# Local attention and feed-forward on one core: first value tiles as 128-row products, wider first queries and keys, masks filled later, a new order

## The chip, the core and the metric

The kernel runs on one core of one Trainium2 chip. The metric is the device time of one execution in microseconds (us), as the median of the runs shown; smaller is better. The engines are TensorE (PE; PEld is its weight load), VectorE (DVE), ScalarE (ACT), GpSimd (POOL) and SyncE (SP, which only issues DMAs here). Each engine executes its own instructions in the order in which the program gives them, and waits for others on semaphores.

## The reference

Everything is bfloat16 with B, S, D = 1, 2048, 448, 16 heads of 28, and F = 1792. The result is x + s * g, where s is an attention over eight dilated positions and g a gated feed-forward, both of the normalised x.

```python
xn = _layernorm(x)                                   # no weights
qkv = (xn @ wqkv).reshape(B, S, 3, H, Dh)            # wqkv: 448 x 1344
idx = pos[:, None] - arange(8)[None, :] * 2          # positions p, p-2, ..., p-14
logits = einsum("bhsd,bhswd->bhsw", q, k[idx]) * Dh ** -0.5   # -1e9 where idx < 0
s = einsum("bhsw,bhswd->bhsd", softmax(logits), v[idx]).reshape(B, S, D) @ wo
h = gelu(xn @ w1 + b1)                               # 448 -> 1792
g = silu(h @ w2 + b2)                                # 1792 -> 448
return x + s * g
```

## The kernel before

**Tokens and tiles.** Tokens are reordered on loading, even positions first and odd ones after, so that the dilated window of a token is itself and the seven before it in its half. There are 16 tiles of 128 tokens; four tiles make a chunk of 512 (chunks 0 to 3). Of the 448 features, three blocks of 128 and one of 64 are contracted.

**Stages.** For each tile: statistics (L422, L426 on DVE), the reciprocal root (L434 on ACT and L437 on DVE for tiles 0 to 3; L443 and L444 on POOL for the others, several tiles together), the normalised `xn` (L456, DVE), and its transpose into `xnT`. For chunk 0 the transpose is done by PE against `ident` (L471) and copied out of the bank by DVE or ACT (L317, L315); later tiles are transposed by a DMA that SP issues (L380). Tile rows of `xn` are 512 wide: DVE copies the last 64 features a second time (L461). Per chunk, `project(c)` then makes values (`vproj`: 128 tokens by 448 columns) and, for four groups `g` of four heads, queries and keys (`qk_cols`: 120 columns by up to 512 tokens, L536). `values(b)` moves pieces of the value tiles into the layout that attention block b wants, by DMAs issued on POOL (L374). The feed-forward has `ff1` (14 products of 128 features by 512 tokens, with a Gelu on ACT, L609) and `ff2` (28 contraction steps, then bias, tanh and products on ACT and DVE). Attention works in nine blocks: scores (L747), exponentials on ACT (L757), a multiplication with a 0/1 mask (`m_gen`, `m_first`, `m_mid`; L764, on DVE or POOL), the product with the values (L780), and the division by the sum through two transposes on DVE (L791 to L805). `final` multiplies by wo (L490, L865), by the gate, adds x (L880) and stores (L884).

**Pairs.** Most products of PE run as 64x64 tiles: `pair(a, b)` works on two products at a time, with four matmuls side by side. In its first phase (16 matmuls) product a uses the upper 64 rows of the contraction and b the lower 64; in the second phase (12 matmuls) it is the other way round. Both write the same two banks, so the second phase waits until the first is done: a no-op on another engine's queue waits for the first phase's last matmul, and the second phase's first matmul waits for the no-op. The program calls it told, here it is the hop:

```python
        def f2(k):
            held["told"] = (nc.gpsimd if k.on == "POOL" else nc.sync).nop()
            behind(held["told"], held["last"][-1])
        told = plan.add(HOPS[0] if early else HOPS[1], 0.06, f2, [t], 300)
```

`HOPS` names POOL for both cases, so each hop stands in POOL's queue behind whatever the order puts ahead of it. In chunk 0 before, a value tile is one pair: its two halves of 224 columns. Queries and keys of groups 0 and 1 are made for 256 tokens at a time there, groups 2 and 3 for 512.

**The order.** `_Plan` is a list scheduler that runs when the program is built. Each step has engines it may run on, an assumed cost, dependences, a priority (`PRIO` by stage, `LATER` added for the steps behind a product) and the buffers it takes and gives (`p_b`: eight PSUM banks). It walks through time and picks, among the steps that could start first, the one of highest priority; steps allowed on two engines go where they would end first. The result is a fixed order on each engine. It also has an assumed delay for blocks of 128 weight-load and matmul pairs (`BLOCK`, `FETCH`). Warm-up matmuls (L330) fill PE until about 8 us in the plan.

**What POOL does at the start.** It fills `ident` (L337), loads b1, fills `own` (L343 to L347), `row0` and `wo` (L322), and then the three masks (L912 to L918), five instructions each; DVE widens the masks to eight copies (L923).

## Time and profile before

| | us |
|---|---|
| median of 3 runs | 161.62 (161.47 to 162.14) |
| profiled execution | 161.79 |
| its span | 160.1 |
| first real product (values of tile 0) on PE | 7.29 |
| first FF1 product on PE | 20.33 |
| first attention scores on PE | 55.00 |
| last matmul issued in the chain | 154.68 to 155.08 |

The profile is of one execution. The page's parts are the busy time of each engine, the span in 40 slices of 4 us (tenths of busy time), DMA queues, the chain of waits that ended last, and groups of instructions. In the chain, a line is start, duration and what was under way; "issue" is time in which the engine waited for nothing that the profile shows. In the list of busy time by stretches, each cell is the busy time of PE, PEld, DVE, ACT and POOL with the number of instructions, then the granted TensorE clock, the share of the DMA engines and GB/s. Names such as L490 are lines of the kernel before; numbers of the changed kernel lie up to 23 higher.

### The profile page before, as it was taken

The numbers are of one execution on the slowest core, as the hardware profiler recorded it, in microseconds if no ns is written. First come the engines' busy times: TensorE is split into PE (matmuls) and PEld (weight loads), VectorE is DVE, ScalarE is ACT, GpSimd is POOL, SyncE is SP. The second block draws the span as 40 slices with busy tenths as digits, with TensorE's granted clock in tenths as the row PEclk, the third lists the DMA queues.
The fourth block names the chain that finished last, engine by engine and source line by source line (L and its number), as shares of the span: only waits on it lengthen the run. The fifth ranks groups of instructions, "written<-read, shape, count | busy, mean of one in ns | idle before, by whom it ended". The sixth has DMA issues, their size and how long they took to land.

```text
span 160.1 us, 7978 instructions
## 1 busy us (share of the span) xinstructions
PE 149.5 (93%) x3535; PEld 100.7 (63%) x3535; DVE 117.8 (74%) x279; ACT 95.3 (60%) x173; POOL 58.8 (37%) x110
## 2 busy tenths in 40 slices
PE   6768699999999999999999999999999999999980
PEld 2456464555555667656987777666677766776570
DVE  6957572248951488988879999999459994597871
ACT  3337279755698773587837478657486598802020
POOL 6856274042382007520256663756003950000000
PEclk9999999999999999999999999999999999999997
DMA  4999469698028532010013230313110000002121
GB/s 144 283 289 316 101 101 121 106 377 277 19 60 128 105 66 80 26 53 4 17 45 95 79 86 14 92 61 104 58 61 4 6 4 4 4 0 61 57 86 33
DMA packets 18707, 14.52 MB, mean 91 GB/s; under 512 B 10037, under 2 KB 17891, under 8 KB 18672
## 3 DMA queue, kind: packets, MB, share of 16 engines
q1 hardware_dynamic: 13200, 7.20, 18.3%
q0 software_dynamic: 2368, 4.06, 11.0%
q10 hardware_dynamic: 3104, 2.75, 5.4%
q8 instruction: 27, 0.44, 1.2%
q14 instruction: 8, 0.07, 0.2%
HBM read 7.06 MB, written 1.84 MB: 56 GB/s over the span
## 4 chain that ended last, share of the span: by engine, by line
PE 81%; DVE 8%; POOL 5%; issue 3%; ACT 1%; POOLq 0%; ACTq 0%; DVEq 0%
PE bank L490 60%; PE bank L536 11%; PE bank L691 3%; PE bank L780 3%; PE bank L747 2%; DVE dt L800 1%; DVE xnT L805 1%; DVE dt L791 1%; DVE y L714 1%; POOL wo L322 1%; DVE g L724 1%; POOL m L916 1%; DVE qT L551 1%; POOL m L918 1%; PE bank L865 1%
## 5 line engine op out<-in xcount | busy, mean ns | idle before, releaser
L490 PE MATMUL bank<-xnT,w 64*64 64x512 bf16 x784 | 44.6, 376 | 0.0
L374 POOL DMA_DIRECT2D v<-v_tok x52 | 27.7, 537 | 44.2 <-PE bank L780 21.2
L490 PE MATMUL bank<-w,h 64*64 64x448 bf16 x784 | 40.4, 349 | 0.1
L609 ACT ACTIVATE h<-bank,b 128x512 bf16<-128x512 f32 x56 | 34.3, 688 | 8.3 <-PE bank L490 8.2
L490 PEld LDWEIGHTS <-w 64*64 64x64 bf16 x784 | 24.3, 107 | 16.5
L490 PEld LDWEIGHTS <-h 64*64 64x64 bf16 x784 | 25.2, 107 | 10.7 <-issue 0.2
L536 PE MATMUL bank<-xnT,w_in 64*64 64x512 bf16 (+1 forms) x504 | 28.2, 353 | 0.2
L549 ACT ACTIVATE qT<-bank,own 128x512 bf16<-128x512 f32 (+1 forms) x24 | 14.8, 651 | 11.4 <-PE bank L536 7.7
L536 PEld LDWEIGHTS <-w_in 64*64 64x64 bf16 x504 | 16.0, 107 | 7.9 <-issue 0.8
L720 ACT ACTIVATE t<-y 128x448 f32<-128x448 f32 x15 | 8.4, 578 | 19.4 <-DVE y L714 19.4
L757 ACT ACTIVATE E<-bank 128x456 bf16<-128x456 f32 (+1 forms) x36 | 17.0, 554 | 4.1 <-PE bank L747 4.1
L490 PEld LDWEIGHTS <-xnT 64*64 64x64 bf16 x408 | 13.3, 106 | 8.2 <-issue 2.5
L490 PE MATMUL bank<-w_in,xnT 64*64 64x448 bf16 (+1 forms) x280 | 14.4, 314 | 3.3 <-issue 1.8
L791 DVE STREAM_TRANSPOSE dt<-bank 128x480 f32<-128x480 f32 (+1 forms) x18 | 12.1, 670 | 4.5 <-PE bank L780 4.5
L764 POOL TENSOR_TENSOR E<-E,m_gen 128x456 bf16<-128x456 bf16 x10 | 10.3, 1054 | 12.0 <-ACT E L757 10.8
L800 DVE STREAM_TRANSPOSE dt<-rd 128x480 f32<-128x480 f32 (+1 forms) x18 | 12.1, 675 | 0.6
L456 DVE TENSOR_SCALAR xn<-x_sb,mv,rstd 128x448 bf16<-128x448 bf16 x16 | 6.6, 411 | 6.4 <-DMA xnT<-xn 4.0
L317 DVE CAST v_tok<-bank 128x448 bf16<-128x448 f32 (+1 forms) x8 | 4.3, 564 | 8.9 <-PE bank L490 8.9
L764 DVE TENSOR_TENSOR E<-E,m_gen 128x456 bf16<-128x456 bf16 (+1 forms) x22 | 9.1, 428 | 2.3 <-ACT E L757 2.0
L551 DVE TENSOR_SCALAR qT<-bank,own 128x512 bf16<-128x512 f32 (+1 forms) x12 | 7.6, 658 | 3.7 <-ACT qT L549 3.7
L714 DVE TENSOR_TENSOR y<-bank,b 128x448 f32<-128x448 f32 x15 | 8.7, 614 | 2.0 <-PE bank L490 1.4
L422 DVE BATCH_NORM_STATS2 st<-x_sb 128x6 f32<-128x448 bf16 x16 | 9.6, 605 | 0.8 <-DMA x_sb<-in_A_x_dram 0.8
(74 smaller groups left out, 165.1 us busy)
## 6 DMA issues: line engine op xcount, KB each, us to landing
v<-v_tok POOLq DMA_DIRECT2D x20, 96.0 KB, 3.1
out_dram<-o SPq DMA_DIRECT2D x15, 112.0 KB, 1.7
w<-in_B_w_dram ACTq DMA_DIRECT2D x2, 784.0 KB, 5.5
w<-in_B_w_dram SPq DMA_DIRECT2D x2, 672.0 KB, 9.2
x_sb<-in_A_x_dram ACTq DMA_DIRECT2D x2, 448.0 KB, 4.5
w_in<-in_A_wqkv_dram SPq DMA_DIRECT2D x4, 168.0 KB, 4.0
w<-in_B_w_dram SPq DMA_DIRECT2D x4, 112.0 KB, 8.5
x_sb<-in_A_x_dram SPq DMA_DIRECT2D x1, 448.0 KB, 7.0
```

What stands on the lines that cost most here:

```text
L374: nc.gpsimd.dma_start(dst(k), src())
L422: nc.vector.bn_stats(out=buf(p_st, k)[:], in_=x_sb[:, t, :])
L490: return [lambda c=c: nc.tensor.matmul(out[c:c + n], lhsT[:, c:c + n], rhs, start=start, stop=stop) for c in range(0, P, n)]
L536: return [lambda i=i: nc.tensor.matmul(ps[64 * i:64 * i + 64, :n], w[:, 2 * DH * i:2 * DH * i + 64], xnT[r, kt, cs], start=start, stop=sto ...
L549: nc.scalar.activation(qT[:, z, g, cs], buf(p_b, o, i)[:, :n], ACT.Copy, scale=own[:, z:z + 1])
L551: nc.vector.tensor_scalar(qT[:, z, g, cs], buf(p_b, o, i)[:, :n], own[:, z:z + 1], None, op0=ALU.mult)
L609: nc.scalar.activation(buf(p_h, own, i)[:], buf(p_b, own, i)[:], ACT.Gelu_apprx_tanh, bias=b1[:, mt:mt + 1])
L714: nc.vector.tensor_tensor(out=buf(p_y, k)[:, :n], in0=buf(p_b, own, i)[:, :n], in1=b2[:, cs], op=ALU.add)
L757: nc.scalar.activation(buf(p_E, k)[:, :n], buf(p_b, a, hl)[:, :n], ACT.Exp, scale=SCALE)
L764: (nc.gpsimd if k.on == "POOL" else nc.vector).tensor_tensor(out=E, in0=E, in1=m[:, :, :nq], op=ALU.mult)
L791: nc.vector.transpose(buf(p_dt, k)[:, :32 * m], buf(p_b, po, w)[:, :32 * m])
L800: nc.vector.transpose(buf(p_dt, d)[:, :32 * m].rearrange("p (b c) -> p b c", c=32), buf(p_rd, r)[:, :m].unsqueeze(2).to_broadcast((P, m, 32)))
```

## The change

Values of tiles 0 to 3 are made by the new `whole`: four matmuls of 128 rows (the last of 64) by 448 columns into one bank, one phase, no hop. The transposes of these tiles put the last 64 features twice into the bank themselves (five transposes instead of four), so DVE's second copy goes; tile 3 is normalised on ACT, with a small DVE product `nb` for its bias; the copies of `xnT` no longer wait for one another. In chunk 0 only group 0 of queries and keys is made in 256 tokens, group 1 now in 512. The loads of x tiles 2 and 3 both come before the query and key weights. The masks and the zero fill of `wo` wait for the fourth `xnT` tile in the plan, and come behind other steps on POOL. The warm-up plans 30 matmuls, the later ones of 256 columns instead of 128. `FETCH` and all numbers of `PRIO` and `LATER` are new, so the order changes everywhere. The tables are cut below.

```diff
--- before.py
+++ after.py
@@ -15,7 +15,7 @@
 SLACK = 0.12
 TABLE = 1.28
 SWITCH = 0.095
-BLOCK, FETCH = 128, ((0.0, 4.6), (40.0, 3.8))
+BLOCK, FETCH = 128, ((0.0, 5.4), (25.0, 4.0))
 SAME = 20
 HOPS = ("POOL", "POOL")
 MASK_ON = (("DVE", "POOL"), (0.4, 1.2))
@@ -253,6 +253,7 @@
     mv = sb("mv", [P, NT, 2], F32)
     sd = sb("sd", [P, NT], F32)
     rstd = sb("rstd", [P, NT], F32)
+    nb = sb("nb", [P, TPC], F32)
 
     def ring(name, n, shape, dt=BF16, fifo=False):
         return _Pool([sb(f"{name}{i}", shape, dt) for i in range(n)], fifo)
@@ -276,25 +277,26 @@
 
 
     PRIO = {
-        "qk": (39.5, 4, 213, 51, 92.5, 143, 200.5, 98, 50.5, 202, 197, 18, 151, 102.5, 140, 200.5,),
-        "values": (173, 201, 102, 152,),
...
+        "qk": (55.5, 79.5, 32, 67, 121.5, 80, 198.5, 81, 54.5, 156, 58, 3, 55.5, 172.5, 116.5,
+            115,),
+        "values": (126.5, 59, 64.5, 123,),
...
-    LATER = {"swap": 99.5, "qk": 74.5, "v": 42.5, "gelu": 77.5, "exp": -10.5, "mask": -47, "pv": 67.5, "recip": 33.5, "os": 175, "y": 205.5, "tanh": 154, "g": 68.5, "sg": 70.5, "o": 26.5}
+    LATER = {"swap": 125.5, "qk": 45, "v": 77, "gelu": 172, "exp": 192.5, "mask": -41.5, "pv": 83.5, "recip": 148.5, "os": 161.5, "y": 154, "tanh": 103, "g": 19.5, "sg": 58.5, "o": 206}
     plan = _Plan()
 
@@ -325,10 +327,10 @@
     warm = p_h.bufs[-1]
     t_on = plan.add("DMA", 0.8, lambda _: None, (), 100)
     t_warm = plan.add("DVE", 0.3, memset("vector", warm[:], 0.0), [t_on], prio=100)
-    for i in range(48):
-        def fn(k, n=512 if i < 9 else P):
+    for i in range(30):
+        def fn(k, n=512 if i < 9 else 256):
             nc.tensor.matmul(buf(p_b, k)[:, :n], warm[:, :P], warm[:, :n], start=True, stop=True)
-        t_warm = plan.add("PE", 0.43 if i < 9 else 0.107, fn, [t_warm], -1, take=(p_b,), limit=8.0)
+        t_warm = plan.add("PE", 0.43 if i < 9 else 0.215, fn, [t_warm], -1, take=(p_b,), limit=8.0)
         t_warm.give = ((p_b, t_warm, 0),)
     t_eps = plan.add("DVE", 0.07, memset("vector", eps_t[:], EPS), [t_on], prio=99)
     t_eps = plan.add("DVE", 0.07, memset("vector", half_t[:], -0.5), [t_eps], prio=99)
@@ -345,7 +347,6 @@
             nc.gpsimd.affine_select(out=own4[:], in_=own4[:], compare_op=ALU.is_ge, fill=0.0, base=op_base,
                                     pattern=[[-sign * DH, 2], [-sign * 64, 2]], channel_multiplier=sign)
         nc.gpsimd.tensor_tensor(out=own[:], in0=own4[:, :, 0], in1=own4[:, :, 1], op=ALU.add)
-    t_own = plan.add("POOL", 0.5, mk_own, [t_on], prio=94)
 
     def heads(v):
         return v.rearrange("p a (b c) -> p a b c", c=32)[:, :, 0:3:2, :]
@@ -358,7 +359,7 @@
 
     t_row0 = plan.add("POOL", 0.1, memset("gpsimd", row0[:], 0.0), [t_on], prio=93)
     t_row0 = plan.add("POOL", 0.1, memset("gpsimd", row0[:1, :], 1.0), [t_row0], prio=93)
-    t_wo = [plan.add("POOL", 1.0, memset("gpsimd", wo[:], 0.0), [t_on], prio=93)]
+    t_own = plan.add("POOL", 0.9, mk_own, [t_row0], prio=94)
 
     def dma(eng, dst, src, kb, prio, deps=(), issue=0.5, rate=350.0, tail=1.7, pieces=1):
         def fn(_):
@@ -405,7 +406,8 @@
             dma("ACT", w_in3[64:], tails[:, 1:3, :], 112, 298, rate=290.0, tail=1.45)]
     t_wqk = []
     for i in range(2):
-        load_x(2 + i, 1, 297 - 2 * i, "SP")
+        load_x(2 + i, 1, 297, "SP")
+    for i in range(2):
         t_wqk.append([load_w(w_in[:, :, c0:c0 + D // 2], A_wqkv[:KF, c0:c0 + D // 2], 296 - 2 * i) for c0 in (i * D // 2, D + i * D // 2)])
 
     t_b1z = plan.add("POOL", 0.1, memset("gpsimd", b1r[:], 0.0), [t_on], prio=99)
@@ -449,38 +451,46 @@
     def half_bank(ap):
         return ap[:].bitcast(BF16)[:, :512].rearrange("p (a b) -> p a b", a=4)
 
-    t_xT, t_xT01 = {}, {}
+    t_xT = {}
 
     def norm(t, prio):
         def f1(k):
             nc.vector.tensor_scalar(buf(p_xn, k)[:, :D], x_sb[:, t, :], mv[:, t, 0:1], rstd[:, t:t + 1],
                                     op0=ALU.subtract, op1=ALU.mult)
-        a = plan.add("DVE", 0.40, f1, [t_rs[t]], prio, take=(p_xn,))
+
+        def f0(_):
+            nc.vector.scalar_tensor_tensor(out=nb[:, t:t + 1], in0=mv[:, t, 0:1], scalar=-1.0, in1=rstd[:, t:t + 1], op0=ALU.mult, op1=ALU.mult)
+
+        def f1a(k):
+            nc.scalar.activation(buf(p_xn, k)[:, :D], x_sb[:, t, :], ACT.Identity, bias=nb[:, t:t + 1], scale=rstd[:, t:t + 1])
+        if t == 3:
+            a = plan.add("ACT", act(D), f1a, [plan.add("DVE", 0.12, f0, [t_rs[t]], 280)], prio, take=(p_xn,))
+        else:
+            a = plan.add("DVE", 0.40, f1, [t_rs[t]], prio, take=(p_xn,))
 
         def f2(_):
             nc.vector.tensor_copy(buf(p_xn, a)[:, D:], buf(p_xn, a)[:, KF:D])
-        twice = plan.add("DVE", 0.15, f2, [a], prio)
         if t >= TPC:
+            twice = plan.add("DVE", 0.15, f2, [a], prio)
             t_xT[t] = dma_T(xnT[:, :, t * P:(t + 1) * P], lambda: buf(p_xn, a)[:], [twice], PRIO["turn_x"][t], (p_xn, a, 0))
             return
         halves = []
         for i in range(2):
             def f3(k, i=i):
                 xn, tp = buf(p_xn, a), half_bank(buf(p_b, (halves or [k])[0]))
-                for kt in (2 * i, 2 * i + 1):
-                    nc.tensor.transpose(tp[:, kt, :], xn[:, kt * P:(kt + 1) * P], ident[:])
-            halves.append(plan.add("PE", 0.13 if t else 0.22, f3, [twice if i else a, t_ident] + halves, prio, take=() if i else (p_b,),
+                for kt, c0, n in ((0, 0, P), (1, 0, P)) if not i else ((2, 0, P), (3, 0, 64), (3, 64, 64)):
+                    nc.tensor.transpose(tp[c0:c0 + n, kt, :], xn[:, kt * P:kt * P + n], ident[:])
+            halves.append(plan.add("PE", (0.13 if t else 0.22) + 0.06 * i, f3, [a, t_ident] + halves, prio, take=() if i else (p_b,),
                                    give=((p_xn, a, 0),) if i else (), tail=0.15, pairs=2))
         b = halves[0]
 
         n = 2 if t < 2 else 4
+        done = []
         for k0 in range(0, KT, n):
             def f4(k, k0=k0):
                 copy(k.on, xnT[:, k0:k0 + n, t * P:(t + 1) * P], half_bank(buf(p_b, b))[:, k0:k0 + n, :])
-            t_xT[t] = plan.add(("DVE", "ACT"), (dve(n * P, 2), act(n * P)), f4, [halves[(k0 + n - 1) // 2]] + ([t_xT01[t]] if k0 else []), prio,
-                               give=((p_b, b, 0),) if k0 + n == KT else ())
-            t_xT01.setdefault(t, t_xT[t])
-
+            done.append(plan.add(("DVE", "ACT"), (dve(n * P, 2), act(n * P)), f4, [halves[(k0 + n - 1) // 2]], prio))
+        t_xT[t] = plan.add("SEM", 0.0, None, done, give=((p_b, b, 0),), tail=-HOP)
 
     def half_rows(half):
         return slice(64 * half, 64 * half + 64) if half < 2 else slice(0, P)
@@ -523,6 +533,13 @@
         a.evac(u, t, 0)
         b.evac(u, t, 1)
         return u
+
+    def whole(j, prio):
+        def f(k):
+            for kt in range(KT):
+                j.part(buf(p_b, k), kt, 2 if kt < 3 else 0, kt == 0, kt == 3)[0]()
+        a = plan.add("PE", pe(j.n, KT), f, j.deps + j.late, prio, take=(p_b,), tail=0.15, pairs=KT)
+        j.evac(a, a, 0)
 
     t_qk = [[] for _ in range(NT)]
 
@@ -566,6 +583,8 @@
         def part(ps, kt, half, start, stop):
             r = half_rows(half)
             w = w_in[r, kt, 2 * D + c0:2 * D + c0 + n] if kt < 3 else w_in3[r, 1, c0:c0 + n]
+            if t < TPC:
+                return [lambda: nc.tensor.matmul(ps[:, :n], xnT[r, kt, k0:k0 + P], w, start=start, stop=stop)]
             return strips(ps[:, :n], xnT[r, kt, k0:k0 + P], w, half, start, stop)
 
         def evac(a, own, i):
@@ -906,6 +925,32 @@
     rstds(4, 2)
     rstds(6, 2)
 
+    blocks_of = [[b for b, (q, n, _) in enumerate(VIS) if (q + 4 * n - 1) // CH == c] for c in range(NCH)]
+
+    def project(c):
+        pv = PRIO["values"][c]
+        for t in range(c * TPC, (c + 1) * TPC):
+            norm(t, PRIO["norm"][t])
+        for t in range(c * TPC, (c + 1) * TPC, 1 if not c else 2):
+            if c:
+                pair(vproj(t, pv), vproj(t + 1, pv), pv - 0.1 * (t % TPC), c < 2)
+            else:
+                whole(vproj(t, pv), pv - 0.1 * t)
+        for g in range(G):
+            q = PRIO["qk"][G * c + g]
+            for t in (range(0, TPC, 2) if not c and g < 1 else (c * TPC,)):
+                pair(*[qk_cols(w, g, t, CH // 2 if not c and g < 1 else CH, q) for w in range(2)], q - 0.1 * (t > 0), c < 2)
...
+    project(0)
+
+    t_wo = [plan.add("POOL", 1.6, memset("gpsimd", wo[:], 0.0), [t_xT[3]], prio=70)]
     t_mask = []
     for m, w1_, n, first in ((m_gen, m1[0], NW, None), (m_first, m1[1], NW, 0), (m_mid, m1[2], NW - 1, 1)):
         def fn(_, s=w1_, n=n, first=first):
@@ -917,34 +962,12 @@
                                         pattern=[[-1, n]], channel_multiplier=1)
                 nc.gpsimd.affine_select(out=a, in_=a, compare_op=ALU.is_ge, fill=0.0, base=BACK - back,
                                         pattern=[[1, n]], channel_multiplier=-1)
-        t_m = plan.add("POOL", 0.9, fn, [t_ident], prio=75)
+        t_m = plan.add("POOL", 1.45, fn, [t_xT[3]], prio=75)
 
         def fn(_, m=m, s=w1_, n=n):
             nc.vector.tensor_copy(m[:, :, :n], s[:, :n].unsqueeze(1).to_broadcast((P, 8, n)))
         t_mask.append(plan.add("DVE", 0.3, fn, [t_m, t_st[3]], prio=60))
 
...
-        for t in range(c * TPC, (c + 1) * TPC, 1 if not c else 2):
-            a = ((t, pv, 0, D // 2), (t, pv, D // 2, D // 2)) if not c else ((t, pv), (t + 1, pv))
-            pair(*[vproj(*j) for j in a], pv - 0.1 * (t % TPC), c < 2)
-        for g in range(G):
-            q = PRIO["qk"][G * c + g]
-            for t in (range(0, TPC, 2) if not c and g < 2 else (c * TPC,)):
-                pair(*[qk_cols(w, g, t, CH // 2 if not c and g < 2 else CH, q) for w in range(2)], q - 0.1 * (t > 0), c < 2)
...
-    project(0)
```

## The prediction

> **What bounds the kernel now.** I read the page first: its table of busy time, then the 40 slices.
>
> ```profile
> PE 149.5 (93%) x3535; PEld 100.7 (63%) x3535; DVE 117.8 (74%) x279; ACT 95.3 (60%) x173; POOL 58.8 (37%) x110
> ...
> PE   6768699999999999999999999999999999999980
> ...
> POOL 6856274042382007520256663756003950000000
> PEclk9999999999999999999999999999999999999997
> ```
>
> TensorE (PE) bounds the kernel: from slice six to the last two it never shows less than 9 tenths, at full granted clock. Time can come from two places: idle PE in the first five slices, or less PE work. So I next took the busy time by stretches (span's start to PE's first wait, and so on; each cell is busy us and count).
>
> ```profile
> 0.00:9.55 9.55, 5.86 (x47) 2.83 (x47) 6.99 (x37) 3.29 (x8) 7.41 (x30) 1.00 0.81 217
> 9.55:15.56 6.01, 6.01 (x177) 4.75 (x178) 4.50 (x15) 3.67 (x12) 3.39 (x7) 1.00 1.07 325
> 15.56:17.35 1.79, 0.00 (x1) 0.00 (x1) 0.99 (x2) 1.13 (x2) 0.52 (x1) 1.00 0.97 184
> 17.35:22.02 4.67, 4.67 (x116) 3.41 (x119) 2.95 (x9) 1.89 (x4) 2.20 (x5) 1.00 0.17 46
> 22.02:150.00 127.98, 127.56 (x3154) 85.31 (x3147) 97.06 (x205) 84.03 (x146) 45.24 (x69) 1.00 0.30 72
> ```
>
> In the body, 22.02 to 150, PE is idle for 0.42 us of 128; in the head one stretch of 1.79 us has no PE work at all, and before 9.55 only 47 matmuls ran, most of them warm-up. The chain of waits says why.
>
> ```profile
> 8.12 0.25 POOL m L918
> ...
> 9.21 0.23 POOL m L916
> 9.44 0.04 issue
> 9.48 0.03 POOLq L515
> 9.50 0.04 issue
> 9.55 0.86 PE bank L490 x28
> ...
> 15.47 0.09 PE bank L490
> 15.56 1.79 issue
> 17.35 0.48 PE bank L490 x11
> ```
>
> The first value pair ran its first phase at 7.29 to 7.8; its second waits for a no-op on POOL (the hop, L515), which stands in POOL's queue behind the fills of three masks (5.34 to 9.44). At 15.56 PE waits for nothing the profile shows. The page's list of DMA queues has a hint.
>
> ```profile
> q8 instruction: 27, 0.44, 1.2%
> q14 instruction: 8, 0.07, 0.2%
> ```
>
> These 0.51 MB over the span's 7978 instructions are 64 bytes each, and a packet of q8 (0.44 MB / 27 = 16 KB) is 256 instructions, 128 pairs of weight load and matmul. The stall falls at PE's pair 224, in the stretch where data DMA is fullest (share 1.07 just before). I read it as a late block of instructions; blocks then change at pairs 95, 223, 351.
>
> **What goes.** Values of tiles 0 to 3 were 4 x 28 matmuls 64x224 and become 4 x 4 of 128x448. Old price by the chain: 0.86 to 0.67 us for 28. New price: the nearest row is L691, 128x448, 14 in 2.75 us, 0.196 each, 0.79 a tile. So this edit saves no PE work (-0.1 to +0.1 a tile, nought taken); it removes four hops and 96 pairs. Group 1 of queries and keys at 512 columns removes 28 pairs and no streaming time (16 of 256 columns take 0.44, 16 of 512 take 0.86). Altogether 120 fewer pairs stand in the head, so the block boundary of pair 224 falls in FF1, whose 512-column matmuls last twice as long per pair.
>
> **The head, step by step** (order of each engine's instructions in the changed kernel, durations from rows before). x0's statistics, root and reciprocal are as now, to 4.76. Two rows of the timeline, of POOL and of DVE:
>
> ```profile
> 3.80 1.58 POOL L322 MEMSET wo<- 128x1792 bf16 x1
> ```
>
> ```profile
> 4.80 0.72 DVE L456 TENSOR_SCALAR xn<-x_sb,mv,rstd 128x448 bf16<-128x448 bf16 x1
> ```
>
> The other three normalisations of chunk 0 took 0.39 to 0.40; this one lay under the memset, which now comes later, so 0.40 is taken. In front of it DVE does an aggregate and two memsets (0.35): xn0 at 5.5, as now. Tile 1 follows at 6.1 (6.86 now, its 0.18 copy gone). ACT turns both into xnT by 7.3 (four copies, 0.33). Values 0 and 1 run from 6.5 to 8.1, behind 16 warm-up matmuls instead of 22 (PE kept clock 1.00 through gaps of 1.47 and 1.79 us; the longest below is 0.65). Their weights were used at 7.29 before, and by 4.0 us from issue at 1.25 to 1.85 land by 6.
>
> Tile 3 is now loaded ahead of the query/key weights, which are issued 0.54 later (its issue row) and land about 8.6 (issue 4.1 to 4.6 plus 4.0); phase one of group 0 takes 0.44, to 9.05. Its hop stands behind POOL's first value move, which waits for ACT's copy of value 0 (8.95: after the roots of tiles 2 and 3 at 8.35) and takes 0.55. So PE waits to 9.6 behind the transposes of tile 2 (9.05 to 9.4), runs phase two to 9.95, and the fifth transpose a tile costs 0.07 (8 took 0.55). Tile 3 is normalised on ACT (0.55 by a copy of 448 columns), behind two value copies: 10.1; transposes to 10.5, values 2 to 11.3. xnT3 stands on DVE behind a query copy that waits for ACT: 11.45; values 3 to 12.25; transposed b1 0.16. Group 1's weights are issued as now (5.2 at the latest, landing by 9.7), so they are there. Then 16+16+12 of 512 (2.37), 16 of 256 (0.44), 12 of 512 (0.65): FF1 starts at 15.9, instead of 20.33. Behind it are left 12 of 256 and one group of 28 (1.85 us); before, 24 of 256 (0.65). Gain: 20.33 + 0.65 - 15.9 - 1.85 = **3.2 us**.
>
> **What is given back.** (1) FF1's third pair needs bank 171, whose key copy DVE now does behind statistics of tiles 4, 5 and 7 (landed 14.45), two mask copies and a query copy: 14.45 + 2.2 + 0.3 + 0.7 + 0.3 + 0.65 = 18.6. PE is there at 17.96: **0.65** lost. (2) PE changes between 64x64 and 128-row products 12 times after its first values instead of 5 after 9.55 (the last six tiles' FF2 parts are interleaved with pairs). Eight transposes between pairs took 0.55 where 8 x 0.053 is 0.43, the one of b1 0.16: 0.05 to 0.06 a switch; the head's are in the rows used, six more in the tail make **0.3**. The Trainium skill, "TensorEngine Tiling (Array Packing)", Key Properties, says that changing the tiling mode drains TensorE: it speaks against this change, gives no figure, and free switches would leave 0.3 more.
>
> (3) Masks moved: 15 POOL instructions (5.34 to 9.74, 1.4 to 1.6 a mask) and wo's memset now follow five value moves, at 11.7 to 17.6. Behind them in that queue stand the hops of groups 1 and 2 and of the second 256 pair, one after each mask, at 13.2, 14.65 and 16.05; PE wants them at 14.1, 15.2 and 16.8. Then rstd of tiles 4 and 5 at 18.7. The cover is 0.6 us at least, so nothing is charged; each us by which POOL is later than that is a us of PE. Masks are first used after attention starts (55 now). The Trainium skill, "SBUF — State Buffer", Who interferes with whom, lets a POOL instruction shut out a VectorE one that uses both ports; the 0.72 row agrees, with 0.32 of it. By that rule the moved fills would cost at most the like once, since DVE has only short mask copies (0.27 to 0.34) of that kind under them.
>
> (4) Tiles 4 to 7 are still turned by SP (1.3 each, landing 3.7 from issue). xn4 comes at 20.2 as now, but xn7 by 22.5 instead of 25.8, so they land at 24.6 to 28.5; PE wants tiles 4 and 5 at 26.1, tiles 6 and 7 at 29.6. The margin is 0.2 and 1.1, no more.
>
> (5) ACT must have FF1's table (1.28) before its Gelus: 17.95 + 1.28 = 19.25, then 0.69 each, two in 1.38 against 1.5 of PE for a pair. It keeps up.
>
> (6) The body's order is new throughout. Its PE work is the same, and only 0.4 us idle and a slow place at 69.2 (16 matmuls in 1.53 instead of 0.86, 1.0 in all with what follows, behind DVE's outputs) could be better; eight mask products go from DVE to POOL (8 x 1.05 more there, 8 x 0.41 less on DVE), four final additions come back, and with the copies that change engine DVE has about 2 us less in all. Bounds: -1.0 (that place goes) to +8.4 (each mask holds a hop). I take 0, because ten such masks and 52 moves now share POOL's queue with the hops and the waits of PE name one hop, the first.
>
> Sum: 3.2 - 0.65 - 0.3 = **2.3 us**. The profiled execution took 161.79 us (span 160.1), 0.17 over the median of 161.62; its span would be 157.8 and its time 159.5, the median **159.3 us**. The tail after the last FF2 part (activation, two multiplications, addition, output) has the same links.
>
> **Rivals.** *Better by the body* (0.15): DVE's 2 us of relief removes the place at 69.2 and bank 171 comes in time: 1.6 more, 157.7. For it: attention starts after FF2 of fewer tiles, so more filler is left. Against: POOL's masks are slower (1.05 for 0.43).
> *The block is still late* (0.13): the block behind pair 95 took from 10.9 to 17.35, 6.45 us. Now pair 95 is reached at 13.1 and pair 223 at about 19.9, 6.8 later, so no stall; a block that comes a full 1.3 us later, say, gives 160.6.
> *PE waits for what feeds it* (0.10): if tiles 4 to 7 or the Gelus come no earlier than now, PE catches up with them at 26 to 30 and the whole gain is a wait: 161.6. Against: (4) and (5).
> *POOL's queue becomes the bound* (0.12), slower than before: hops of the pairs stand behind 18 masks of 1.05 instead of 10. It decides from 3.1 us of the 8.4 exposed (2.3 + 0.8); half exposed gives 159.3 + 4.2 = 163.5. Against: the single hop wait in 52 moves.
>
> **Numbers.** Forecast 0.50; with the first two rivals faster has 0.78, same 0.10, slower 0.12. About 0.8 us (0.5%) is what can be told from no change. The range, 157.5 to 161.8, holds all but the POOL case and the farther ends.
>
> **What would show it.** Right: no PE wait on a POOL hop before 9; no issue wait of over 0.5 us; first FF1 product at 15.5 to 16.5; a PE wait of about 0.6 on DVE's key copy at 18; PE's last matmul near 152.8 instead of 155.1. Wrong: FF1 after 18, or a body (FF1's start to the last matmul) with over 2 us of PE idle, above all behind POOL.

## The result: slower by 1.1%

The changed kernel takes **163.67 us** (median of 4 runs, 162.97 to 163.96) against 161.70 (161.47 to 162.14) for the kernel before beside it: a ratio of **1.0112** (95% interval 1.0073 to 1.0151). The forecast was 159.3, range 157.5 to 161.8. The profiled execution took 163.78, its span is 161.7. Some executions run a few us longer than the others of the same kernel; the ratios leave these out, the medians do not.

Page of the changed kernel, busy time and slices:

```profile
PE 153.1 (95%) x3409; PEld 103.1 (64%) x3409; DVE 121.3 (75%) x270; ACT 93.0 (57%) x168; POOL 63.6 (39%) x114
...
PE   6999889999999989999999999999999899999990
...
POOL 6047669262452880760589427532003550000000
```

PE has fewer instructions (3409 for 3535) and more busy time. The head is fuller, as forecast; but PE shows 8 tenths at slices 5 and 6 (16 to 24 us), 15 and 32, where the kernel before had 9 in every slice behind the fifth up to the last two. By stretches (cells as before):

```profile
0.00:7.56 7.56, 6.31 (x27) 3.00 (x28) 5.86 (x33) 2.90 (x7) 2.57 (x14) 1.00 0.76 204
7.56:9.47 1.91, 1.91 (x10) 0.59 (x7) 0.80 (x5) 1.32 (x5) 0.02 (x1) 1.00 1.01 283
9.47:17.11 7.64, 7.57 (x121) 3.98 (x124) 3.25 (x10) 3.85 (x8) 5.53 (x19) 1.00 1.01 296
17.11:22.02 4.91, 3.71 (x73) 2.11 (x69) 4.84 (x10) 3.43 (x6) 3.02 (x5) 1.00 0.08 21
22.02:150.00 127.98, 126.16 (x3085) 88.08 (x3081) 98.97 (x199) 79.64 (x140) 52.42 (x77) 1.00 0.32 75
```

FF1 starts at 17.11 (20.33 before), with no wait for a hop and no issue wait ahead of it. But PE is idle for 1.20 us from there to 22, and for 1.82 us of the 128 behind, where it was 0.42. The chain of waits at the first place:

```profile
17.72 1.65 DVE m_first L968
19.37 0.54 DVE st L424
19.91 0.02 issue
19.93 0.18 DVE mv L428
20.11 0.58 DVE kT L319
20.70 0.04 issue
20.74 7.53 PE bank L500 x135
```

PE's third FF1 pair waits for DVE's key copy (L319), and that stands behind a copy of a mask of which 1.65 us lie in this chain. (L968 is L923 of the kernel before: the lines of the mask fills and copies lie 45 higher, not up to 23.)

Busy time hides small waits, so for the rest I use one more measure: the time from each matmul's start to the next one's, less its streaming time at full clock (columns / 2400 us, a quarter of it for a 64x64 tile; the prediction's 0.86 for sixteen of 64x512 is this to within 0.01). I call the sum **excess**. It also holds the 2.5 to 2.6 us that the attention's short products (64x57) take beyond their columns, before and after alike, so what counts are differences between kernels.

| kernel | 0 to 20 us | 20 to 145 | after 145 | sum | last matmul starts |
|---|---|---|---|---|---|
| before | 7.59 | 5.69 | 0.31 | 13.59 | 155.19 |
| changed | 6.48 | 7.58 | 0.89 | 14.95 | 157.20 |

The last matmul starts 2.01 later: 0.64 of more streaming (values of four tiles 0.37, transposes 0.21, warm-up 0.05), 1.10 less excess in the head, 1.89 more in the body, 0.58 more in the tail. All later ratios are to the kernel before, run beside the same kernels.

### The profile page after: what moved, and what is told of

It is laid out like the page before. It is cut to its first block, busy times and chain, and to the rows that moved or that the text cites. A ratio compares the mean times of both kernels' runs of the same rounds, so it can differ in the third digit from the quotient of the medians.

```text
span 161.7 us, 7710 instructions
## 1 busy us (share of the span) xinstructions
PE 153.1 (95%) x3409; PEld 103.1 (64%) x3409; DVE 121.3 (75%) x270; ACT 93.0 (57%) x168; POOL 63.6 (39%) x114
## 4 chain that ended last, share of the span: by engine, by line
PE 73%; DVE 19%; ACT 3%; issue 2%; DVEq 0%; ACTq 0%
PE bank L500 48%; PE bank L553 11%; PE bank L710 3%; PE bank L332 3%; DVE dt L819 3%; PE bank L799 2%; DVE dt L810 2%; PE bank L587 2%; DVE y L733 2%; DVE w_in L743 2%; DVE E L783 1%; DVE sg L893 1%; DVE qT L568 1%; DVE xnT L824 1%; ACT E L776 1%
## 5 line engine op out<-in xcount | busy, mean ns | idle before, releaser
L500 PE MATMUL bank<-xnT,w 64*64 64x512 bf16 x784 | 46.4, 376 | 1.5 <-DVE kT L319 1.2
L500 PE MATMUL bank<-w,h 64*64 64x448 bf16 x784 | 41.1, 349 | 0.0
L500 PEld LDWEIGHTS <-w 64*64 64x64 bf16 x784 | 27.5, 107 | 16.4 <-issue 3.2
L553 PE MATMUL bank<-xnT,w_in 64*64 64x512 bf16 (+1 forms) x476 | 30.2, 364 | 0.5 <-DVE xnT L824 0.5
L783 POOL TENSOR_TENSOR E<-E,m_gen 128x456 bf16<-128x456 bf16 x17 | 18.6, 1120 | 23.1 <-ACT E L776 20.0
L568 DVE TENSOR_SCALAR qT<-bank,own 128x512 bf16<-128x512 f32 (+1 forms) x18 | 12.5, 714 | 14.1 <-PE bank L553 8.2
L566 ACT ACTIVATE qT<-bank,own 128x512 bf16<-128x512 f32 (+1 forms) x16 | 10.1, 659 | 11.5 <-PE bank L553 8.6
L500 PEld LDWEIGHTS <-xnT 64*64 64x64 bf16 x296 | 10.9, 107 | 4.9 <-issue 1.2
L500 PE MATMUL bank<-w_in,xnT 64*64 64x448 bf16 x168 | 10.8, 350 | 0.6 <-DVE xnT L824 0.6
L317 ACT CAST kT<-bank 128x512 bf16<-128x512 f32 (+1 forms) x15 | 8.3, 553 | 2.9 <-PE bank L500 2.3
L317 ACT CAST v_tok<-bank 128x448 bf16<-128x448 f32 x12 | 6.0, 541 | 4.9 <-issue 2.3
```

Of the source, the lines that this page charges most:

```text
L317: nc.scalar.copy(o, i)
L500: return [lambda c=c: nc.tensor.matmul(out[c:c + n], lhsT[:, c:c + n], rhs, start=start, stop=stop) for c in range(0, P, n)]
L553: return [lambda i=i: nc.tensor.matmul(ps[64 * i:64 * i + 64, :n], w[:, 2 * DH * i:2 * DH * i + 64], xnT[r, kt, cs], start=start, stop=sto ...
L566: nc.scalar.activation(qT[:, z, g, cs], buf(p_b, o, i)[:, :n], ACT.Copy, scale=own[:, z:z + 1])
L568: nc.vector.tensor_scalar(qT[:, z, g, cs], buf(p_b, o, i)[:, :n], own[:, z:z + 1], None, op0=ALU.mult)
L783: (nc.gpsimd if k.on == "POOL" else nc.vector).tensor_tensor(out=E, in0=E, in1=m[:, :, :nq], op=ALU.mult)
```

## The experiments

Two theories stood first. *Blocking*: POOL's moved memset and its eight additional mask products shut DVE out, and DVE's late copies hold PE's banks. *Order*: the new order's queue on DVE holds PE, whatever POOL does. Apart from experiments 10 and 11, every kernel keeps the finished order and moves, adds or leaves out only the named steps in it.

**1. The memset of wo in front again.**

```diff
     plan.run()
+    t_wo[0].deps = []
+    t_wo[0].start = t_own.start + 0.01
+    plan.order.sort(key=lambda t: (t.start, t.seq))
```

> One move in the changed kernel: the memset of wo goes back to the front of POOL's queue (right behind own), everything else in the same order. If POOL's memset is what held VectorE's copy of m_first (1.74 us where the other copies took 0.27) and through it the key copy that frees bank 171: m_first's copy takes 0.27 to 0.34, PE's wait of 1.21 in FF1 at 19.2 is gone or below 0.2, PE's last matmul comes 1.2 to 1.5 us earlier (157.2 to 155.8) and the time is 162.2 to 162.5. If VectorE's new order alone makes the key copy late: the wait stays at 0.7 or more and the time at 163.0 to 163.7. If the wait goes but a later one (tiles 4 and 5 at 26 to 31) takes it over: no wait at 19, a new one of about 1 us before 32, time 163.5.

162.72 us, ratio 1.0074 (1.0045 to 1.0102): 0.4% better than the changed kernel, less than the first expectation. DVE's timeline of the changed kernel, POOL's, and DVE's of this one:

```profile
17.63 1.74 DVE L968 COPY m_first<-m 128x456 bf16<-128x456 bf16 x1
```

```profile
17.65 1.59 POOL L324 MEMSET wo<- 128x1792 bf16 x1
```

```profile
17.30 0.27 DVE L968 COPY m_first<-m 128x456 bf16<-128x456 bf16 x1
17.49 0.62 DVE L424 BATCH_NORM_STATS2 st<-x_sb 128x6 f32<-128x448 bf16 x1
18.14 0.18 DVE L428 BATCH_NORM_AGGREGATE mv<-st 128x2 f32<-128x6 f32 x1
18.25 0.66 DVE L319 CAST kT<-bank 128x512 bf16<-128x512 f32 x1
```

The copy that ran beside the memset ended 0.13 after the memset's end; without it the copy takes 0.27, and the wait at 19 (excess 1.53) is gone. The third expectation came true in part: PE now waits at 29.8 (excess 0.84) for a DMA transpose of tiles 4 to 7.

**2. Besides, value tiles in one mode.**

```diff
-                j.part(buf(p_b, k), kt, 2 if kt < 3 else 0, kt == 0, kt == 3)[0]()
+                j.part(buf(p_b, k), kt, 2, kt == 0, kt == 3)[0]()
...
+                w = w if kt < 3 else w_v3[:]
...
```

> The kernel of the run before (memset of wo in front), and the last of the four products of each value tile 0 to 3 also takes 128 rows: its weights lie in a tile of their own whose lower 64 rows are zero (one more DMA on ACT's queue and one memset at the start), so TensorE keeps one mode through a value tile. If changing from 128 to 64 rows and back costs a drain: the fourth product takes 0.19 to 0.20 instead of 0.285 and the first of the next tile 0.19 instead of 0.29, 0.2 a tile; FF1 starts 0.4 to 0.8 us earlier than in the run before (tile 3's normalisation may eat half) and the time falls by 0.4 to 0.8, to about 161.8. If the two long products are long for another reason (clock, weights landing): they stay at 0.28 and the time is that of the run before within 0.2.

162.74 us, 1.0068 (1.0043 to 1.0094). PE's timeline of the changed kernel, then of this one:

```profile
7.56 1.99 PE L587 MATMUL bank<-w_in,xnT 128*128 128x448 bf16 x8
9.47 0.63 PE L553 MATMUL bank<-xnT,w_in 64*64 64x256 bf16 x16
```

```profile
7.08 0.73 PE L592 MATMUL bank<-w_in,xnT 128*128 128x448 bf16 x3
7.65 0.35 PE L592 MATMUL bank<-w_v,xnT 128*128 128x448 bf16 x1
7.84 0.73 PE L592 MATMUL bank<-w_in,xnT 128*128 128x448 bf16 x3
8.41 0.35 PE L592 MATMUL bank<-w_v,xnT 128*128 128x448 bf16 x1
8.69 0.63 PE L557 MATMUL bank<-xnT,w_in 64*64 64x256 bf16 x16
```

Two tiles took 1.91 from start to start of the next work, and now 1.61; the second tile's first product starts 0.19 after the fourth of the first (7.84 after 7.65). So in these rows a 64-row product in a stream of 128-row products costs as a change of mode does, 0.1 on the way in and 0.1 on the way out. FF1 starts 0.67 earlier than in experiment 1, of which 0.14 is an earlier first product; the time does not change. PE's excess is now 0.49 and 0.60 in waits for DVE at 17 to 19, and 1.08 in the wait for the transposes at 30.

**3. POOL's masks left out.**

```diff
-                (nc.gpsimd if k.on == "POOL" else nc.vector).tensor_tensor(out=E, in0=E, in1=m[:, :, :nq], op=ALU.mult)
+                if k.on == "DVE":
+                    nc.vector.tensor_tensor(out=E, in0=E, in1=m[:, :, :nq], op=ALU.mult)
```

> The changed kernel with the 18 mask products that POOL does left out (those weights stay unmasked, so part of the attention mask is missing); VectorE's are kept, and the order too. If PE's waits in the body come from VectorE being shut out by POOL's mask products: VectorE's instructions at 51.6, 53.2, 129.3 and 130.5 are back at their usual times, PE's waits at 59.7 (0.94) and 133.0 (0.62) go, and the time falls by 1.2 to 1.6, to 162.1 to 162.5. If VectorE's in-order queue alone makes them (four softmax denominators and outputs in a row ahead of the bank's release): they stay, as those at 68.0 (0.82) and 126.4 (0.71) do by either theory, and the time stays within 0.3 of 163.7.

161.43 us, 0.9993 (0.9970 to 1.0017): 1.2% better than the changed kernel, somewhat more than expected. Body excess falls from 7.58 to 6.10, of 1.89 that the change had added; another 0.6 of this profile's gain lies in the head, where the program is the same (last section). The waits at 126 and 133 both go, also the one that blocking did not claim; that at 59.7, which it did claim, keeps 0.58 of 0.94, and that at 68 keeps 0.77 of 0.82. So POOL's masks are most of the body's loss. That they cause it by blocking alone is not shown by this: leaving them out also spares the products that wait for a mask. Experiment 6 tries to part the two.

**4. One part of the change in the kernel before: mask fills late.**

```diff
     plan.run()
+    for i, m in enumerate(t_mask):
+        m.deps[0].start, m.start = 23.0 + 0.01 * i, 33.0 + 0.01 * i
+    plan.order.sort(key=lambda t: (t.start, t.seq))
```

> The kernel before, with one part of the change alone: POOL's fills of the three masks (15 instructions) and VectorE's copies of them are moved to about 23 and 33 us, the rest in the same order. The wait of 1.63 for the hop at 7.9 goes by either theory. If the block of instructions behind pair 224 comes about 6.4 us after the block before it was begun: both move forward, the idle time at 15 stays near 1.8 and the time falls by 1.3 to 1.6, to 160.0 to 160.4. If the block comes at a time of its own (17.3, behind the data loads): the idle time at 15 grows to about 3.3 and the time stays at 161.4 to 161.8. What could halve the gain in both: a wait for weights of queries and keys, landing at about 8.6.

160.97 us, 0.9969 (0.9943 to 0.9995). PE's waits:

```profile
PE bank L490 <- issue: 1.6, 1, 1.6
PE bank L330 <- DVE eps_t L322: 1.2, 1, 1.2
PE bank L490 <- POOLq L515: 1.0, 1, 1.0
```

The hop's wait at 7.9 is gone. The issue wait stays and ends at 15.79 instead of 17.35, with pair 95 reached at 9.40 instead of 10.78. From pair 95 to pair 223 it is 6.6 us in the kernel before, 6.4 here and 5.6 in experiment 8: the late block of instructions moves with the one before it, as the forecast had read, though not at a fixed distance (experiment 13). But 1.0 (excess 1.34) returned at 26.9, where a hop now stood behind the fills I had moved.

**5. On experiment 2 ("the last run but two" in the text below): the feed of tiles 4 to 7 earlier.**

```diff
...
+    at(14.03, *t_st[4].deps, t_st[4])
+    at(17.05, *t_st[7].deps, t_st[7])
+    at(18.31, *norms[5], *norms[4])
+    t_rs[4].start = 18.30
```

> The kernel of the last run but two (memset of wo in front, value tiles in one mode) with what feeds tiles 4 to 7 moved up in the queues: VectorE's statistics of tile 4 ahead of those of tile 7, its three mask copies behind 24 us, the normalisations of tiles 5 and 4 ahead of the statistics of tile 6, and POOL's root of tiles 4 and 5 one hop earlier. There the time was 162.74 although FF1 began 0.67 us earlier, with waits of 0.25, 0.28 and 0.76 at 17.7, 19.2 and 31.2. If the gain of the head was lost to the feed of tiles 4 to 7 (four transposes by DMA, one behind the other on SP, 5.4 us, plus 3.2 to landing): the first transpose starts at 19.2 to 19.8 instead of 21.03, the wait at 31 shrinks from 1.08 to below 0.3, those at 17 to 19 by half, the last matmul comes 1.0 to 1.6 us earlier and the time is 161.2 to 161.8. If the time lost lies in the body or in the spread of the executions: the waits before 32 shrink but the time stays at 162.5 to 162.9.

162.85 us, 1.0079 (1.0049 to 1.0108): a miss. The waits at 17 to 19 go, but PE waits 1.18 (excess 1.51) for a transpose at 31.0:

```profile
PE bank L504 <- DMA xnT<-xn: 1.2, 1, 1.2
```

The first transpose starts at 19.86, the fourth still ends its issue at 26.45, since tiles 6 and 7 are normalised no earlier, and one of the trace's transposes lands 5.7 after its issue (shortest 2.5).

**6. Six of POOL's masks done by DVE**, those that ran beside stretched DVE instructions.

```diff
+    on_pool = [t for t in plan.order if t.on == "POOL" and len(t.eng) == 2 and t.cost == MASK_ON[1]]
+    for i in (1, 2, 9, 10, 17, 18):
+        on_pool[i].on = "DVE"
```

> The changed kernel with six of POOL's mask products (the 2nd, 3rd, 10th, 11th and the last two, which ran at the same time as VectorE instructions that took 0.27 to 0.86 longer than their like) done by VectorE at the same place in the order; nothing is left out. Leaving out all of POOL's masks brought 1.2%. If VectorE's being shut out is what cost that: VectorE takes on 6 x 0.40 = 2.4 us and is rid of 3.4, PE's waits at 126.4 (0.71) and 133.0 (0.62) go, that at 59.7 shrinks, and the time is 162.0 to 162.7. If it was the mask work itself (on whichever engine, weights come later to their products): the time stays at 163.4 or rises by up to 1.

163.06 us, 1.0085 (1.0046 to 1.0123), 0.3% better than the changed kernel: less than expected, and the intervals do not tell it from nothing. DVE's rows of the changed kernel at two of the places, POOL's at one, and the same two steps of DVE in this kernel:

```profile
53.23 1.02 DVE L472 COPY xn<-xn 128x64 bf16<-128x64 bf16 x1
...
130.50 1.47 DVE L743 SCALAR_TENSOR_TENSOR w_in<-t,y 128x448 bf16<-128x448 f32 x1
```

```profile
53.17 2.52 POOL L783 TENSOR_TENSOR E<-E,m_gen 128x456 bf16<-128x456 bf16 x2 [1.07 <-PE bank L553]
```

```profile
53.17 0.18 DVE L472 COPY xn<-xn 128x64 bf16<-128x64 bf16 x1
...
129.65 0.62 DVE L743 SCALAR_TENSOR_TENSOR w_in<-t,y 128x448 bf16<-128x448 f32 x1
```

With the six on DVE all such stretches of 0.5 and more in the body are gone, as is the wait at 133; that at 126 stays (0.72), since DVE's own four steps of a softmax output are ahead of it. The body's excess falls by 0.64 only, from 7.58 to 6.94: DVE is rid of 3.7 us of stretching (0.2 and more above the lower quartile of the same line and form) and takes on 6 masks of 0.4. So the stretching is shown, and one wait that it made; how much of experiment 3's 1.48 it is, and how much the mask work itself, is not.

**7. All of these together** (1, 2, 5 and 6).

> The first two kernels of this call in one: memset of wo in front, value tiles in one mode, feed of tiles 4 to 7 earlier, six masks on VectorE; nothing is left out. If the four costs found so far add: 163.7 - 1.0 (memset) - 0.7 (modes) - 0.3 (feed, beyond making the 0.7 count) - 1.2 (masks) = 160.2 to 160.9, ahead of the kernel before (161.5) by 0.4 to 0.8%. If each only moves the wait on to the next engine: 161.5 to 162.3.

162.17 us, 1.0019 (0.9990 to 1.0048): the upper case. The costs do not add: a wait for a transpose (1.05 at 30.7, excess 1.38) takes back much of what the head won.

**8. Experiment 4 with the fills at 29, 34 and 38 us**, the copies at 42.

```diff
+    for m, fill, copied in zip(t_mask, (29.25, 34.33, 38.25), (42.0, 42.1, 42.2)):
+        m.deps[0].start, m.start = fill, copied
```

> The kernel before with the fills of the three masks moved to 29, 34 and 38 us, one at each place, where POOL was idle, and VectorE's copies of them to 42. With the fills at 24 they held a hop at 26.9 (PE's wait 1.34) and the time was 160.97. If that wait was the fills' alone: it goes and the time is 159.6 to 159.9. If tiles 4 to 7 come no earlier than about 28.5 to 30 in this order (transposes issued from 19.3, 7.1 us for four): PE waits there for a DMA instead, 0.8 to 1.3, and the time stays at 160.6 to 161.0.

**160.00 us, 0.9920 (0.9898 to 0.9942).** Page, PE's and POOL's slices:

```profile
PE   6997999999999999999999999999999999999970
...
POOL 6354581272870018500366634845005840000000
```

The 1.0 at 26.9 was the fills' alone, and in the old order the transposes come in time. POOL's timeline has the fills at 30.6 to 32.0, 35.9 to 37.2 and 39.8 to 41.1; in the kernel before POOL had nothing to do from 26.5 to 34.2 and from 37.0 to 42.4 (its value moves in between come at 32.6 to 35.3 here). PE waits for no hop now.

**9. Experiment 7 with four loads moved behind the transposes** (x of tiles 8 to 15 and w2, on ACT's queue).

```diff
+    for i, d in enumerate((t_x[8], t_w2[0][0], t_x[12], t_w2[1][0])):
...
+        d.start = 30.37 + 0.01 * i
```

> The kernel that joined the four corrections (162.17) and, besides, the four loads on ACT's queue (x of tiles 8 to 15, w2; 2.4 MB) moved behind ACT's next key copy, from 26.0 to about 29.8. There PE waited 1.05 at 30.7 for a transpose by DMA that was issued by 25.7 but landed 5.7 us after its issue, where the shortest took 2.5. If the loads that start at 26.0 slow the last transposes: tile 7 lands by 29, PE's wait falls below 0.4, the last matmul comes 0.9 to 1.3 us earlier and the time is 160.9 to 161.3. If the transposes are slow on their own (one behind the other, or beside POOL's moves of values): the wait stays at 0.8 or more and the time at 161.9 to 162.3. If chunk 2's statistics, now 4 us later, come late: a new wait at 50 to 60.

162.07 us, 1.0021 (0.9991 to 1.0052). The excess at 29.5 falls from 1.38 to 0.45, but waits of 0.73 at 17 and 0.36 at 54 appear, and the time stays. One profile can't settle whether the loads slow the transposes: in experiment 14 the wait was absent with the loads where they had been.

**10 and 11. Code and numbers crossed:** the changed code with the old `PRIO`, `LATER` and `FETCH`, and the old code with the new ones.

> The changed kernel's code (value tiles as 128-row products, group 1 at 512 columns, masks filled later, tile 3 on ACT) with the priorities, delays and block table of the kernel before; the planner makes a new order from them. If the parts of the change are a gain and only the new order's collisions and waits lose it (memset under a copy 1.5, masks under VectorE 1.9, tail 0.3): 160.3 to 161.5, below the kernel before or equal. If the parts themselves cost (modes 0.7, feed no earlier): 161.8 to 163.5. An order drawn from numbers that were chosen for other code may be worse by up to 2 us for no reason of the parts; the waits in its body tell.

> The kernel before with the priorities, delays and block table of the changed one: the new order's numbers alone. If the new numbers are what makes the body wait (VectorE under POOL's masks, four softmax steps ahead of a bank's release): waits of 0.5 to 1.0 at several places between 50 and 140, 2 us or more in all against 3.5 of excess before, and 162.5 to 165. If the numbers do no harm by themselves: 161.0 to 162.0.

177.41 us, 1.0912 (1.0850 to 1.0973), and 171.53 us, 1.0559 (1.0504 to 1.0614). Both expectations are far off, and nothing follows for the parts. What they show is the weight that an order can have: one drawn from numbers that were chosen for other code costs 6 to 9% here. The forecast put the new order at nought, with +8.4 us as its upper bound.

**12. Experiment 8 with value tiles as 128-row products in one mode** (8 of 128x224 a tile, no hop; the same `w_v3`).

```diff
+            if a.n == D // 2:
+                held["last"] = [j.part(ps, kt, 2, kt == 0, kt == 3)[0]() for j, ps in ((a, p), (b, q)) for kt in range(4)]
+                return
```

> The kernel before with its mask fills at 29 to 38 us (160.0), and besides the value tiles 0 to 3 as 128-row products in one mode (8 of 128x224 a tile in two banks, all where the first phase stood; the last weights in a tile of their own whose lower 64 rows are zero): the first part of the change alone, in the old order. Streaming costs 8 x 0.093 = 0.75 a tile where 28 x 0.0233 = 0.65 was, and four groups between 64x64 products cost a change of mode each way, 0.1 to 0.2: 0.25 a tile, 1.0 in all. It also has 80 pairs of weight load and matmul fewer, so the block boundary at pair 224 moves out of the head into FF1 and the idle time of 1.04 at 13.9 should go. By this the two cancel: 159.7 to 160.3. If 128-row products are a gain in themselves (no hop, fewer weight loads), or modes are free: 158.9 to 159.4. If the block comes late all the same, behind a pair further on: 160.7 to 161.2.

159.89 us, 0.9915 (0.9881 to 0.9949), beside 0.9920 without it. This is what the first expectation gave for parts that cancel: in the old order this part of the change is worth nothing, within 0.4%. The one profile is of its longest run (165.06 us, with a load of x that landed at 18.4), so the parts themselves are not seen.

**13. Experiment 8 with the memset of wo on DVE at 25 us.**

```diff
+    t_wo[0].fn = memset("vector", wo[:], 0.0)
+    t_wo[0].start = 25.0
```

> The kernel before with its mask fills at 29 to 38 us (160.0), and besides the memset of wo taken from POOL at 3.8 to VectorE at about 25, where VectorE was idle. If POOL's memset is what stretched the first normalisation from 0.40 to 0.64 to 0.72: it takes 0.40, tile 0 is transposed 0.2 to 0.3 earlier and the time is 159.6 to 159.8. If what follows waits for the arrival of the weights or the second tile in any case: 160.0 within 0.15.

**159.37 us, 0.9865 (0.9824 to 0.9907)**, the fastest kernel here and a little more than expected, though its interval and experiment 8's overlap. DVE's row for the first normalisation, 0.72 long before:

```profile
4.70 0.40 DVE L456 TENSOR_SCALAR xn<-x_sb,mv,rstd 128x448 bf16<-128x448 bf16 x1
```

Tile 0 is transposed 0.40 earlier than in experiment 8 (5.16 for 5.56). But this profile also lacks that kernel's issue wait (0.8 at 14.98): pair 223 starts 5.15 after pair 95, with no wait, so how late the block comes differs from 5.15 or less to 6.6 in the old order, and the gain is not all the normalisation's.

**14. Experiment 7 with two of DVE's copies on ACT**, at 53.9 and 62.2.

```diff
+    for i in (435, 493):
+        plan.tasks[i].on = "ACT"
+    plan.tasks[493].start = 60.48
```

> The kernel that joined the four corrections (162.17, 1.002 of the kernel before) with two of VectorE's copies, a query copy at 53.9 (0.75) and a value copy at 62.2 (0.61), done by ScalarE, which had idle time of 1.1 to 1.9 there; nothing else moves. VectorE had no idle time from 50.9 to 60.3 and from 61.5 to 68.4, and PE's waits at 58.4 (0.71) and 66.6 (0.77) end with its last step of a softmax output. If VectorE's queue in the new order is what makes these waits: the first falls to 0.1 or less, the second to 0.3, and the time by 0.8 to 1.2, to 161.0 to 161.4. If PE only waits for another bank instead, of ScalarE's now longer queue: the waits move by a few us and the time stays at 161.9 to 162.4.

The last line also moves the second copy's place in the plan, to 60.48. 161.04 us, 0.9978 (0.9944 to 1.0011), an interval that overlaps experiment 7's. PE's timeline of experiment 7, then of this one:

```profile
66.55 0.37 PE L557 MATMUL bank<-xnT,w_in 64*64 64x512 bf16 x1
67.38 2.57 PE L557 MATMUL bank<-xnT,w_in 64*64 64x512 bf16 x43 [0.45 <-DVE xnT L829]
```

```profile
65.32 2.85 PE L557 MATMUL bank<-xnT,w_in 64*64 64x512 bf16 x44
```

The wait at 66.6 is gone, that at 58 keeps 0.59 of 0.71. The wait for the transposes is absent too, in the same order up to there, so their landing differs between executions. Of the 1.76 of excess that this profile has less than experiment 7's, 1.1 is that and 0.7 lies between 55 and 75, where the copies are. So this one profile shows the order's load on DVE at one of the two places.

| kernel | 0 to 20 us | 20 to 145 | after 145 | sum | ratio |
|---|---|---|---|---|---|
| changed | 6.48 | 7.58 | 0.89 | 14.95 | 1.0112 |
| 1 memset first | 4.70 | 8.27 | 0.76 | 13.74 | 1.0074 |
| 3 no masks on POOL | 5.85 | 6.10 | 0.63 | 12.58 | 0.9993 |
| 7 all together | 4.24 | 8.18 | 0.65 | 13.07 | 1.0019 |
| 14 two copies on ACT | 4.30 | 6.39 | 0.61 | 11.31 | 0.9978 |
| 8 before, fills late | 5.49 | 5.74 | 0.35 | 11.59 | 0.9920 |
| 13 and memset on DVE | 4.94 | 5.76 | 0.27 | 10.98 | 0.9865 |

Each row is one profile, and up to 0.7 in the head column is not the program's (last section). Kernels with the new code also stream 0.64 more. Experiment 7 differs from 8 by that, by a tail longer by 0.3, and by 2.4 of body excess, against 1.3 won in the head.

## Why the prediction was wrong

PE's last matmul was forecast near 152.8 and came at 157.20, 4.4 later. The head's sum makes 1.2 of that, bank 171 0.6, the body 1.9 and the tail 0.3; 0.4 is not placed. So the largest failed step is (6), the body put at nought.

**Right.** The late block, and that fewer pairs would move it out of the head; no hop wait before 9; no issue wait over 0.5; that the moved fills free the first hop (experiment 8: this part alone, with the fills put where POOL was idle, brings 0.8%).

**The head's sum** was too early by 1.2: FF1 at 17.11 for 15.9. The first value product came at 7.56 for 6.5. In experiments 3 and 6, whose program is the same up to there, it came at 6.83 and 7.41, so up to 0.7 of that is not the program's (last section). Part of it is, though. PE's warm-up ahead of the first transposes in the kernel before and in the changed one, and DVE's row for tile 0 in the latter:

```profile
1.24 3.79 PE L330 MATMUL bank<-h 128*128 128x512 bf16 x12 [1.24 <-DVE eps_t L322]
```

```profile
1.25 4.88 PE L332 MATMUL bank<-h 128*128 128x512 bf16 x13 [1.25 <-DVE eps_t L324]
```

```profile
5.10 0.26 DVE L458 TENSOR_SCALAR xn<-x_sb,mv,rstd 128x448 bf16<-128x448 bf16 x1
```

Tile 0 was normalised at 5.36, earlier than the forecast's 5.5, but PE was still at its warm-up, now with four matmuls of 256 columns at the end instead of three of 128, and turned to the transposes at 5.91. At the start 512 columns take 0.427 from start to start, twice the 0.213 of full clock; the page's 1.00 does not show this, and the forecast gave the warm-up no price. The value tile was priced at 0.79 from a row of 14 equal products; it took 0.96, because its last product has 64 rows and changes the mode twice. Step (2) counted changes between 64x64 and 128 only. Behind the first two value tiles the head ran as forecast, within 0.2.

**Step (1)**, 0.65 for bank 171, measured 1.21; without the memset it is nought.

**Step (3) is the first that failed, and by its size.** It charged nothing and took "the like" of 0.32 as the most a moved fill could cost, from the normalisation that took 0.72 beside the memset. But that instruction had begun at 4.80, with 0.58 of the memset (3.80 to 5.38) left; it simply ended 0.14 after it. In both rows the price of such a meeting goes by what is left of POOL's instruction: 0.32 of 0.58 there, and here, with all 1.59 left, 1.47 above the usual 0.27. Experiment 1 shows it. The Trainium skill, "SBUF — State Buffer", Who interferes with whom, calls it an exclusive lock; the rows agree, and the step used the rule without taking the lock's length from it.

**Step (6) failed as a whole.** Eight more masks on POOL were weighed by hops behind them (nought to 8.4) and by relief of DVE (2 us). PE waited for no hop, and DVE's busy time rose from 117.8 to 121.3: instructions of DVE that met POOL's masks took 0.26 to 0.86 longer. In the whole kernel such stretches (0.2 and more above the lower quartile of the same line and form) sum to 5.5 us, the 1.47 of step (3) among them, for 2.4 before. Experiment 3 gives the masks 1.2% of the time (its one profile has an early head besides); how much of this is stretching and how much the mask work itself stays open (experiment 6). What experiment 6 leaves at 59, 67 and 126 stands behind DVE's queue in the new order; experiment 14 shows it at one of these places.

**Step (4)** gave tiles 4 and 5 a margin of 0.2 and tiles 6 and 7 one of 1.1. That was nearly the truth and should have capped the sum: with the memset out of the way PE's excess there is 0.84, with one mode 1.08, with the earlier feed 1.51. In these profiles a head that is faster by about a microsecond waits for the transposes; only in experiment 14 did they come in time. The rival *PE waits for what feeds it* had 0.10.

**The slower rival** named 163.5, beside the 163.67 measured, but by another mechanism: hops behind POOL's masks. Here PE's waits end with steps of DVE, not with hops. That the time fits is chance.

One reading was wrong without bearing on the sum: of the 47 matmuls before 9.55 in the kernel before, 22 were warm-up, not most.

**Open:** why the transposes land 2.4 to 6.2 after their issue, why the late block is gone in experiment 13, and the tail's 0.58 (six changes of mode forecast at 0.3), which was not tried.

## What to carry to other kernels

When work moves to GpSimd or to another time on it, list what VectorE does at that time: each instruction of the kind that was stretched here can be held until GpSimd's ends, so long memsets belong where VectorE is idle, or on VectorE itself. Price a change by its parts in the old order before a new order is drawn: here the part that paid, three fills moved to where POOL was idle, was worth 0.8% and the package lost 1.1%. A gain at the start is worth no more than the next feed allows, so look for the transfer that PE meets next.

## What the hardware showed that was not expected

**The clock falls after a long wait.** In experiment 10 PE waited 4.74 us for a transpose. Stretches of its trace (cells as above; the granted clock is the third number from the end):

```profile
28.00:30.00 2.00, 2.00 (x44) 1.11 (x36) 1.16 (x2) 1.72 (x3) 0.00 (x0) 1.00 0.79 104
30.00:35.00 5.00, 0.37 (x8) 0.00 (x0) 0.00 (x0) 0.00 (x0) 0.00 (x0) 0.80 1.17 192
35.00:36.00 1.00, 0.89 (x12) 0.52 (x16) 0.00 (x0) 0.00 (x0) 0.00 (x0) 0.50 1.08 377
...
39.00:40.00 1.00, 1.00 (x16) 0.48 (x12) 0.31 (x1) 0.28 (x1) 0.00 (x0) 0.61 0.70 242
40.00:45.00 5.00, 5.00 (x96) 2.58 (x92) 4.05 (x9) 3.74 (x7) 2.65 (x5) 1.00 0.23 62
```

Sixteen products of 64x512 took 1.92 at 36.6 instead of 1.03; 2.3 us of excess stand behind the wait. Waits of up to 1.79 in the kernel before left the clock at 1.00.

**The start of full speed differs between executions.** PE's ten transposes of tiles 0 and 1, in the changed kernel and in experiment 3, whose program is the same up to there:

```profile
5.91 1.37 PE L482 MATMUL bank<-ident,xn 128*128 128x128 bf16 x10
```

```profile
5.60 0.96 PE L482 MATMUL bank<-ident,xn 128*128 128x128 bf16 x10
```

The page's clock is 1.00 in both, but the clock records of the trace begin at 6.96 in the first and at 5.26 in the second: 0.4 us here, and 0.3 in the warm-up ahead. Over the sixteen profiles of this case they begin at 4.1 to 7.1, with PE's first matmul at 1.24 or 1.25 in each. The Trainium skill, "TensorE: Matmul & The Clock Gate", What's actually happening, has a free-running window of about 3.4 us that sets the clock by how busy PE was; both findings agree with it: the records change in steps of 3.41 us.
